# Attention chunks and a two-layer MLP on one core: v of the first batch loaded chunk by chunk, and the first loads and steps in another order

## The chip, the cores and the metric

The kernel runs on one core of one Trainium2 chip. The metric is device time in microseconds (us). A core has five engines that run side by side, each in the order of its own instructions: TensorE (PE: matrix products and transposes, written to PSUM banks), VectorE (DVE), ScalarE (ACT), GpSimd (POOL, here the issuer of nearly all loads) and SyncE (SP, here the issuer of stores and of DMA transposes). They meet through semaphores: an instruction that waits holds up all behind it on its engine. Loads and stores run on 16 DMA engines.

## The reference

```python
# q, k, v: 8 batches x 8 heads x 576 positions x 64, float32
q_c, k_c, v_c = (a.reshape(B, H, 9, 64, 64) for a in (q, k, v))    # chunks of 64 positions
scores = D ** -0.5 * np.matmul(q_c, k_c.transpose(0, 1, 2, 4, 3))
scores = scores - np.max(scores, axis=-1, keepdims=True)
attn = np.exp(scores)
attn = attn / (np.sum(attn, axis=-1, keepdims=True) + 1e-09)
out = np.matmul(attn, v_c)                                          # attention within a chunk only
x = out.transpose(0, 2, 1, 3).reshape(4608, 512)                    # tokens x (heads * 64)
h = x @ w_in                                                        # 512 x 2048
g = np.maximum(0.01 * h, h)
result = g @ w_out                                                  # 2048 x 512, float32
```

## The kernel before

**Attention units.** The 4608 tokens are cut into 36 units u of 128 tokens (two chunks, all 8 heads). A unit goes through stages, each a small function: `tq`/`tk` transpose q and k on PE, `q`/`k` (later `Q`) copy them from PSUM to SBUF, `s` computes the scores on PE, `m`/`b` take the row maximum and subtract it on DVE, `x` is the exponential on ACT, `z` the sum and its reciprocal, `n` the normalisation on DVE, `e`/`c` transpose the result on PE and copy it (u below 5) or `d` has it transposed by a DMA that SP issues (u of 5 and more), `v` multiplies with v on PE, and `a` copies the product to `xT` on ACT. From u=14 on q and k come as D loads and are transposed on DVE (`dq`, `dk`), and the exponential is fused with the subtraction (`nb`, `f`).

**MLP blocks.** The tokens are also cut into 22 blocks j: eight of 128 and fourteen of 256 tokens. The first layer `mm1(j, a)` (line 262) multiplies `w_inT` with `xT` into a PSUM bank `hT` (a pool of four banks), `act1` (stage G, line 277) puts the leaky ReLU into `gT`. The second layer is `mm2(j, ti, part)` (line 292, four matmuls of 512 columns) or, for blocks 8 to 20, seven half-size products `prod` with sums and differences of halves: `W` forms differences of `w_outT` (line 170) four times in all, `sum` those of `gT`, `comb` joins the products.

**Order.** Every engine's order is the order in which the Python code emits. Three texts and a list set it:

- `LOADS` is the order of the first loads, all issued by POOL on one queue: `gN` is q and k of unit N (lines 87), `vN` is v of batch N (two DMAs, line 109), `QN` a quarter of w_in (512 of its 2048 columns, two DMAs, line 116), `PN` a quarter of w_out (line 128). q and k of u=0 come on the queues of SP and ACT.
- `FRONT` is an order written out by hand for the first units and blocks. `iN` is filler: matmuls of `warm` with itself, N times 128 columns in pieces of up to 384. `yN`, `wN` zero parts of tiles, `I` copies the identity matrix. `Aj.a` is `mm1` of block j with w_in's quarter a, `Gj.a` its activation, `Bj.p` is `mm2` of block j with w_out's quarter p, `Oj` the copy and store of its result. A suffix such as `q1.0.1` names unit, half and engine (the last 1 is ACT).
- After `FRONT`, the remaining groups of matmuls (`chunks`) run one per step; ahead of each, all events due by that step are emitted, and all events up to the one that completes the tokens that the group needs. Event times follow from `T[u]`, the sum of `SPACE` up to u, and from distances: `O_P` (transposes ahead of scores), `O_Q` (DVE transposes ahead of scores), `O_X`, `O_N`, `O_Z` (exponential, normalisation behind scores), `O_U` (v behind scores for u below `U_V`) and `O_V` (from there on), `O_W` and `O_Y` (start and spacing of the four `W`), `O_E` and `O_L` (loads D3 and later), `O_D` (loads g9 to g13), `D_G` and its like for the MLP's own followers.
- v of batch b+2 is loaded into the tile of batch b right behind the last `v` that reads it (line 601's function calls `load_v`).

A load's place in `LOADS` is its place on POOL and on the queue. The tiles of v of the first batch, `VB[0]`, are read chunk by chunk: unit u reads chunks 2u and 2u+1, so u=0 reads 0 and 1, u=3 reads 6 and 7, and u=4 reads chunk 8 and the first chunk of batch 1.

Of the kernel before, what the change touches and what calls it, by code (L numbers as in the profile page):

```python
# [16 lines left out]
def kernel(  # L17
# [9 lines left out]
    nc = tc.nc  # L27

    B, H, S, D = q.shape
# [3 lines left out]
    CH = 64  # L33
# [25 lines left out]
    VB = [sbp.tile([128, H // 2, NCH, 128], FP16, name=f"VB{i}") for i in range(NVB)]  # L59
# [47 lines left out]
    def load_v(b):  # L107
        for m in range(2):
# [2 lines left out]
                in_=v[b, m * H // 2:(m + 1) * H // 2].rearrange("h (c j) d -> j (h c) d", j=CH),  # L111
            )

    def load_w_in(f0, f1):
        for m in range(2):
            nc.gpsimd.dma_start(
                out=w_inT[m * CH:(m + 1) * CH, :, f0:f1],
                in_=moe_w_in[m * d_model // 2:(m + 1) * d_model // 2, f0:f1].rearrange("(t d) f -> d t f", d=D),
            )

    def load_w_in_quarter(a):
        load_w_in(512 * a, 512 * a + 512)
# [11 lines left out]
    for eng, name, src in ((nc.sync, "q_f", q), (nc.scalar, "k_f", k)):  # L134
# [10 lines left out]
    qk[0] = tuple(first)  # L145

    LOADS = (
        "g2 g1 g3 v0 Q0 Q1 Q2 g4 Q3 g5 P1 P2 P0 P3 g6 v1 g7 g8 "
    )
    LOADERS = {"g": load_qk, "v": load_v, "Q": load_w_in_quarter, "P": load_w_out_quarter, "D": load_qk_batch}  # L150
    ident = sbp.tile([128, 128], FP16, name="ident")
    for n, what in enumerate(LOADS.split()):
        LOADERS[what[0]](int(what[1:]))
        if n == 0:
# [99 lines left out]
    def mm1(j, a, p):  # L254
        tb, c0 = part_of(j, p)
        r0 = (START[j] + c0) % RING
        nf = 512 // tb
        hT = psp.tile([128, nf, tb], FP32, name="hT", tag="mm", bufs=4)
        for i in range(nf):
            fc = nf * a + i  # L260
            for t in range(NT):
                nc.tensor.matmul(  # L262
                    out=hT[:, i, :],
                    lhsT=w_inT[:, t, fc * 128:(fc + 1) * 128],
                    rhs=xT[:, t, r0:r0 + tb],
                    start=(t == 0),
                    stop=(t == NT - 1),
                )
        HT[j, a, p] = hT
# [93 lines left out]
    def at(t, *what):  # L363
        now["order"] += 1
        events.append((t, now["order"], what))
        events.sort()
# [6 lines left out]
    def flush(*keys):  # L373

        for e in [e for e in events if e[2][0] in keys]:
            events.remove(e)
            issue(e)

    def later(n, *what):
        at(now["step"] + n, *what)  # L380

    def fill():
        kind, j, a, p = chunks.pop(0)
        if kind == "mm1":
            mm1(j, a, p)
            later(D_G, "G", j, a, p)
        elif kind == "sums":
            flush("G")
            for n, m in enumerate((1, 2, 3, 4)):
                later(n * D_S, "sum", j, m)  # L390
        elif kind == "prod":
# [5 lines left out]
            if p == BLOCKS[j] // 256 - 1:  # L397
                if a == 7:
                    later(D_K, "combX", j, 7)
                    later(D_K, "combZ", j, 5)  # L400
                elif a in (1, 6):
                    later(D_K, "combX", j, a)
                elif a == 4:
                    later(D_K, "combX", j, a)
                elif a == 2:
                    flush("combX")
                    later(D_C, "combW", j, a)
                elif a == 3:
                    later(D_C, "combZ", j, a)
        elif j == len(BLOCKS) - 1 and a == BLOCKS[j] // 128 - 1:  # L410
# [3 lines left out]
        else:  # L414
            flush("G")
            mm2(j, a, p)
            if parts[j, a] == NFC // 4:
                later(D_O, "O", j, a)

    D_G = 1.5  # L420
    D_S = 2.5
    D_K = 0.25
    D_C = 1.0
    D_O = 0

    QP: dict[int, bass.AP] = {}
    KP: dict[int, bass.AP] = {}
# [218 lines left out]
    def zero_act(i):  # L646
# [8 lines left out]
            )  # L655

    FRONT = (
        "i33 y4 y2 I y0 tq0 w3 q0.1.1 y1 tk0 k0 q0.0 i13 s0 m0 b0 tq1 q1.0.1 x0 tk1 q1.1 k1 i11 tq2 s1 z0 "
        "m1 b1 q2.0.1 tk2 q2.1.1 k2 x1 i5 tq3 n0 q3.0.1 i10 e0 c0.1 s2 tk3 z1 m2 v0 q3.1.1 a0 k3 n1 b2 "
        "i12 e1 c1 x2 i5 s3 v1 z2 a1 n2 m3 A0.0 G0.0 A1.0 e2 G1.0 A1.1 c2 v2 a2 b3 A0.1 A2.1 A1.2 x3 G1.1 "  # L660
        "z3 A2.0 G0.1 tq4 n3 G2.0 e3 tk4 c3 G2.1 A2.2 v3 G1.2 A0.2 A2.3 a3 G2.2 A1.3 q4.1 A3.3 G2.3 G0.2 "
        "A3.1 k4 G3.1 q4.0 G1.3 s4 G3.3 tk5 A3.2 y6 tq5 A3.0 m4 A0.3 G3.2 B1.2 G0.3 q5.0 b4 x4 B0.2 G3.0 "
        "B1.1 z4 B0.1 B1.0 B3.0 n4 k5.1 e4 B3.1 B1.3 B0.0 c4 B0.3 O1 q5.1.1 y5 O0 "
    )
    STAGES = {
        "tq": stage_tq, "tk": stage_tk, "q": stage_q, "k": stage_k, "s": stage_s, "m": stage_m, "b": stage_b,
# [25 lines left out]
            done.add((name, how[0]))  # L692
        STAGES[name](*how)

    SPACE = [4.5, 4.5, 5, 6.0, 6.0, 7, 4.5, 6, 6, 6, 7.5, 9.0, 8.5, 8.5, 9.5, 8.0, 7.5, 8.0, 7.0, 10.0, 7.0, 8.5, 7.5, 7.5, 8.5, 6.0, 8.0, 8.0, 9.0, 10.0, 9.0]
    O_P = 4.0
    O_Q = 6.5
    O_R = 1.0
    O_M = 0.5
    O_X = 3.0  # L700
    O_F = 3
    O_H = 0
    O_Z = 5.0
    O_N = 4.0
    O_U = 13.0
    O_V = 16.5
    U_V = 14
    O_L = -1.5
    O_W = 31
    O_Y = 2  # L710
    O_E = 2
    O_D = 4.0
    UY = 10
    T = {5: 0}
    for u in range(6, NU):
        T[u] = T[u - 1] + SPACE[u - 6]
    at(3, "v", 4)
    at(3, "a", 4)
    for u in range(5, NU):
        t = T[u]  # L720
        if u >= UD:
            at(t - O_Q, "dq", u, 0)
            at(t - O_Q + O_R, "dq", u, 1)
            at(t - O_Q + 2 * O_R, "dk", u)
        elif u > 5:
            for what in ("tq", "tk", "Q", "k"):
                at(t - O_P, what, u)
        at(t, "s", u)
        at(t + O_M, "m", u)
        if u < UX:  # L730
            at(t + O_M, "b", u)
            at(t + O_X, "x", u)
            n = t + O_N
        else:
            at(t + O_M, "nb", u)
            at(t + O_F, "f", u, 0, 4)
            at(t + O_F + O_H, "f", u, 4, 8)
            n = t + O_Z
        for what in ("z", "n", "d"):
            at(n, what, u)  # L740
        w = t + (O_U if u < U_V else O_V)
        at(w, "v", u)
        at(w, "a", u)
    for u in range(9, UD):
        at(T[u - 3] - O_D, "g", u)
    for b in range(3, B):
        at(T[9 * b // 2 - 5] - (O_E if b == 3 else O_L), "D", b)
    for n in range(4):
        at(O_W + n * O_Y, "W", n + 1)
    STAGES["Q"] = both  # L750
# [43 lines left out]
```

## Time and profile before

| what | us |
|---|---|
| median of 3 runs | 287.69 (287.58 to 287.98) |
| the profiled execution's own time | 287.43 |
| its span | 285.6 |
| PE busy | 275.5 (96%) |
| DVE busy | 198.3 (69%) |
| ACT busy | 197.3 (69%) |
| POOL busy | 115.2 (40%) |
| filler matmuls, 27 of 384 columns, 3 of 256, 2 of 128 | 8.4 |
| first-layer matmuls (line 262), 1408 | 142.9 |

The span is the time from the first to the last instruction of the profiled execution; its own time holds what lies around it as well. Busy time counts each engine's instructions; PE's includes the filler. A row of a timeline gives the start, the length, the engine, the line, the operation with the tiles it writes and reads, how many instructions are merged, and in brackets the idle time ahead with what ended it. Matmul lengths are modelled and overlap, so starts are the safer thing to count with.

### The profile page before, as it was taken

To read this page: it belongs to the slowest core of one execution; us is meant where nothing else is said; L and a number is where in the kernel's file an instruction comes from. 1 tells how busy PE (TensorE), PEld (TensorE's weight loads), DVE (VectorE), ACT (ScalarE), POOL (GpSimd) and SP (SyncE) were. 2 spreads that over 40 slices of the span, in tenths; PEclk is the share of its full clock that TensorE was granted. 3 is DMA by queue.
4 is the path that set the end of the run, shared out by engine and by line. 5 is a ranking of instruction groups with operands and counts; after the bars stand their busy time and mean duration, and the time that the engine had idled before them with its cause. 6 is when DMAs were issued, how large, how long until landed. Compare 5 with 4: busy or idle time off the path is not lost.

```text
span 285.6 us, 7842 instructions
## 1 busy us (share of the span) xinstructions
PE 275.5 (96%) x3140; PEld 233.8 (82%) x3140; DVE 198.3 (69%) x398; ACT 197.3 (69%) x634; POOL 115.2 (40%) x144
## 2 busy tenths in 40 slices
PE   8779999979999899999999999999999999999995
PEld 4569945777778799999999999999899999988874
DVE  5876245956699998787688886888787968442210
ACT  6856624646557697797788886878888888765431
POOL 8748625747899231963009830983000000000000
DMA  9999999999999939999919999999921212211012
GB/s 148 157 196 169 187 175 196 166 164 127 154 160 156 116 37 171 95 133 92 154 21 142 99 138 97 145 101 141 116 67 21 93 22 92 57 57 52 24 73 75
DMA packets 183332, 32.75 MB, mean 115 GB/s; under 512 B 174336, under 2 KB 178816, under 8 KB 183296
## 3 DMA queue, kind: packets, MB, share of 16 engines
q0 software_dynamic: 158880, 18.23, 121.4%
q1 hardware_dynamic: 23232, 13.70, 21.5%
q8 instruction: 24, 0.39, 0.5%
q10 hardware_dynamic: 1184, 0.33, 0.5%
q14 instruction: 12, 0.10, 0.1%
HBM read 36.96 MB, written 9.44 MB: 162 GB/s over the span
## 4 chain that ended last, share of the span: by engine, by line
PE 75%; DMA 12%; POOL 7%; DVE 4%; issue 1%; ACT 0%; DVEq 0%; ACTq 0%; POOLq 0%
PE hT L262 37%; PE prX L202 16%; PE prZ L202 8%; PE oP L292 5%; DMA q_d<-in_q_dram 5%; PE prW L202 4%; DMA w_inT<-in_moe_w_in_dram 3%; PE xp L601 2%; DMA et<-en 2%; DMA k_d<-in_k_dram 2%; PE Sp L507 2%; POOL k_d L100 2%; DVE TW L170 2%; POOL VB L109 2%; POOL k_in L87 1%; POOL q_in L87 1%
## 5 line engine op out<-in xcount | busy, mean ns | idle before, releaser
L262 PE MATMUL hT<-xT,w_inT 128*128 128x256 f16 (+1 forms) x1408 | 142.9, 253 | 2.0 <-DMA w_inT<-in_moe_w_in_dram 1.3
L262 PEld LDWEIGHTS <-w_inT 128*128 128x128 f16 x1408 | 115.0, 98 | 12.6 <-issue 2.4
L277 ACT ACTIVATE gT<-hT 128x512 f16<-128x512 f32 x144 | 84.4, 617 | 29.3 <-PE hT L262 28.6
L537 ACT ACTIVATE ex<-Sp,nb 128x64 f16<-128x64 f32 x176 | 52.5, 335 | 0.5 <-DVE nb L529 0.4
L100 POOL DMA_DIRECT2D q_d<-in_q_dram x40 | 32.4, 832 | 34.7 <-DVE QZ L489 29.2
L202 PEld LDWEIGHTS <-SG 128*128 128x128 f16 x416 | 40.4, 98 | 4.7
L537 ACT ACTIVATION_READ_ACCUMULATOR ex<-Sp,nb 128x1 f32 x176 | 40.3, 229 | 0.0
L516 DVE TENSOR_REDUCE mx<-Sp 128x8 f32<-128x512 f32 x36 | 24.7, 686 | 13.5 <-PE Sp L507 13.3
L100 POOL DMA_DIRECT2D k_d<-in_k_dram x40 | 32.4, 840 | 3.8 <-DMA q_d<-in_q_dram 3.5
L292 PE MATMUL oP<-w_outT,gT 128*128 128x512 f16 x144 | 33.5, 379 | 0.0
L615 ACT ACTIVATE xT<-xp 128x512 f16<-128x512 f32 x36 | 21.7, 602 | 16.9 <-PE xp L601 16.7
L202 PEld LDWEIGHTS <-gT 128*128 128x128 f16 x312 | 29.4, 98 | 3.2
L489 DVE STREAM_TRANSPOSE QZ<-q_d 64x512 f16<-64x512 f16 (+1 forms) x48 | 31.2, 656 | 0.4
L109 POOL DMA_DIRECT2D VB<-in_v_dram x16 | 18.5, 1168 | 29.6 <-PE xp L601 21.9
L227 DVE TENSOR_TENSOR osb<-prZ,keep 128x256 f32<-128x256 f32 x26 | 10.9, 418 | 25.7 <-ACT keep L218 14.8
L202 PE MATMUL prX<-TW,SG 128*128 128x256 f16 x208 | 27.0, 273 | 0.0
L568 DVE TENSOR_TENSOR en<-ex,zi 128x512 f16<-128x512 f16 x36 | 24.9, 691 | 1.2
L292 PEld LDWEIGHTS <-gT 128*128 128x128 f16 x144 | 13.3, 98 | 13.5
L218 ACT ACTIVATE keep<-prX 128x256 f32<-128x256 f32 x39 | 16.1, 412 | 8.3 <-PE prX L202 7.8
L561 DVE TENSOR_SCALAR ze<-z 128x8 f32<-128x8 f32 x36 | 8.8, 245 | 12.6 <-ACT ex L537 12.1
L183 DVE TENSOR_TENSOR SG<-gT 128x1024 f16<-128x1024 f16 x26 | 17.6, 675 | 0.0
L601 PEld LDWEIGHTS <-VB 128*128 128x128 f16 x288 | 13.0, 98 | 4.1 <-issue 2.3
(67 smaller groups left out, 312.1 us busy)
## 6 DMA issues: line engine op xcount, KB each, us to landing
out_dram<-osb SPq DMA_DIRECT2D x35, 256.0 KB, 3.1
VB<-in_v_dram POOLq DMA_DIRECT2D x16, 288.0 KB, 6.5
q_d<-in_q_dram POOLq DMA_DIRECT2D x40, 72.0 KB, 5.6
k_d<-in_k_dram POOLq DMA_DIRECT2D x40, 72.0 KB, 6.1
w_inT<-in_moe_w_in_dram POOLq DMA_DIRECT2D x8, 256.0 KB, 9.4
w_outT<-in_moe_w_out_dram POOLq DMA_DIRECT2D x4, 512.0 KB, 10.6
q_in<-in_q_dram POOLq DMA_DIRECT2D x11, 128.0 KB, 9.0
k_in<-in_k_dram POOLq DMA_DIRECT2D x11, 128.0 KB, 9.0
```

The costliest lines, as they stand in the source:

```text
L100: nc.gpsimd.dma_start(out=t[p0:p0 + 32, m, :, :, :].rearrange("p h b d -> p (h b) d"), in_=src[b, h0:h0 + 2, :, dh * 32:dh * 32 + 32].rear ...
L109: nc.gpsimd.dma_start(out=VB[b % NVB][m * CH:(m + 1) * CH, :, :, m * CH:(m + 1) * CH].rearrange("p h c d -> p (h c) d"), in_=v[b, m * H // ...
L202: nc.tensor.matmul(out=to[:, i, :], lhsT=left[:, f, i * 128:(i + 1) * 128], rhs=right[:, f, :], start=(j, where) not in opened, stop=(f == ...
L262: nc.tensor.matmul(out=hT[:, i, :], lhsT=w_inT[:, t, fc * 128:(fc + 1) * 128], rhs=xT[:, t, r0:r0 + tb], start=(t == 0), stop=(t == NT - 1),)
L277: nc.scalar.activation(out=gT[j][:, nf * a:nf * a + nf, c0:c0 + tb], in_=HT.pop((j, a, p)), func=AFT.Prelu, bias=0.0, scale=1.0, alpha=0.01,)
L292: nc.tensor.matmul(out=o, lhsT=gT[j][:, fc, ti * 128:(ti + 1) * 128], rhs=w_outT[:, fc, :], start=(n == 0 and fc == part * 4), stop=(n == ...
L489: nc.vector.transpose(out=qz[s * CH:(s + 1) * CH, :, e0:e0 + n, s, :], in_=qkd[b][0][s * CH:(s + 1) * CH, :, at:at + n * CH].rearrange("p ...
L516: nc.vector.tensor_reduce(out=MX[u], in_=SP[u], axis=AXL.X, op=ALU.max)
L537: nc.scalar.activation(out=E[u][:, i, :], in_=SP[u][:, i, :], func=AFT.Exp, bias=NB[u][:, i:i + 1], scale=SCL, accum_out=Z[u][:, i:i + 1],)
L568: nc.vector.tensor_tensor(out=E[u], in0=ex, in1=ZI.pop(u).unsqueeze(2).to_broadcast((128, 8, CH)), op=ALU.mult)
L601: nc.tensor.matmul(out=xp[:, t, e, :], lhsT=VB[b % NVB][:, t, c, :], rhs=et[:, t // 2, e, t % 2, :] if u < UD else et[:, t % 2, e, t // 2, :],
L615: nc.scalar.activation(out=xT[:, :, at:at + G], in_=xp, func=AFT.Copy, bias=0.0, scale=1.0)
```

## The change

One new loader takes a single chunk c of v of the first batch, two DMAs for it (one for each half of the heads). `LOADS` uses it nine times in place of `v0`, spread between the quarters of w_in, with chunk 8 behind v of batch 1; g3 stands behind the first quarter of w_in and three chunks, and the quarters of w_in and w_out come in another order. `FRONT` is written anew with the same stages: the number of filler units and their places differ (73 in place of 89), as does the order of zeroing, copies, first-layer and second-layer groups. Behind `FRONT`, `SPACE` and sixteen distances have other values. For u from 6 to 13, v comes 16.5 steps behind the scores in place of 13, since `U_V` is 6 in place of 14; for u=5 it is 12. The four `W` are due from step 14 on in place of 31, D3 at step 21 in place of 12.

```diff
+    def load_v_chunk(c):
+
+        for m in range(2):
+            nc.gpsimd.dma_start(
+                out=VB[0][m * CH:(m + 1) * CH, :, c, m * CH:(m + 1) * CH],
+                in_=v[0, m * H // 2:(m + 1) * H // 2, c * CH:(c + 1) * CH, :].rearrange("h j d -> j h d"),
+            )
+
     LOADS = (
-        "g2 g1 g3 v0 Q0 Q1 Q2 g4 Q3 g5 P1 P2 P0 P3 g6 v1 g7 g8 "
+        "g2 g1 c1 Q0 c2 c0 g3 Q2 c5 c3 Q1 c4 c7 Q3 g4 c6 g5 P3 P2 P1 P0 g6 v1 c8 g7 g8 "
     )
-    LOADERS = {"g": load_qk, "v": load_v, "Q": load_w_in_quarter, "P": load_w_out_quarter, "D": load_qk_batch}
+    LOADERS = {"g": load_qk, "v": load_v, "c": load_v_chunk, "Q": load_w_in_quarter, "P": load_w_out_quarter, "D": load_qk_batch}
-    D_G = 1.5
-    D_S = 2.5
-    D_K = 0.25
-    D_C = 1.0
-    D_O = 0
+    D_G = 1.25
+    D_S = 2.25
+    D_K = 0
+    D_C = 1.25
+    D_O = 0.75
     FRONT = (
-        "i33 y4 y2 I y0 tq0 w3 q0.1.1 y1 tk0 k0 q0.0 i13 s0 m0 b0 tq1 q1.0.1 x0 tk1 q1.1 k1 i11 tq2 s1 z0 "
-        "m1 b1 q2.0.1 tk2 q2.1.1 k2 x1 i5 tq3 n0 q3.0.1 i10 e0 c0.1 s2 tk3 z1 m2 v0 q3.1.1 a0 k3 n1 b2 "
-        "i12 e1 c1 x2 i5 s3 v1 z2 a1 n2 m3 A0.0 G0.0 A1.0 e2 G1.0 A1.1 c2 v2 a2 b3 A0.1 A2.1 A1.2 x3 G1.1 "
-        "z3 A2.0 G0.1 tq4 n3 G2.0 e3 tk4 c3 G2.1 A2.2 v3 G1.2 A0.2 A2.3 a3 G2.2 A1.3 q4.1 A3.3 G2.3 G0.2 "
-        "A3.1 k4 G3.1 q4.0 G1.3 s4 G3.3 tk5 A3.2 y6 tq5 A3.0 m4 A0.3 G3.2 B1.2 G0.3 q5.0 b4 x4 B0.2 G3.0 "
-        "B1.1 z4 B0.1 B1.0 B3.0 n4 k5.1 e4 B3.1 B1.3 B0.0 c4 B0.3 O1 q5.1.1 y5 O0 "
+        "y0 y4 i46 I tq0 w3 tk0 q0.1.1 y1 y2 k0 q0.0 s0 m0 tq1 q1.0.1 tk1 k1 b0 x0 q1.1 tq2 z0 s1 q2.1.1 m1 "
+        "b1 q2.0.1 i3 tk2 k2 x1 tq3 i7 i13 n0 q3.0.1 e0 tk3 s2 i2 c0.1 z1 m2 k3 v0 b2 q3.1.1 i2 n1 s3 a0 x2 "
+        "m3 e1 c1 z2 v1 a1 n2 A0.0 b3 A1.0 e2 G1.0 A1.2 x3 c2 v2 G0.0 A1.1 A0.1 z3 n3 a2 A2.1 G1.2 e3 G0.1 "
+        "c3 A2.0 G1.1 tk4 v3 A2.2 k4 A0.2 tq4 G2.0 a3 A3.3 A2.3 q4.1 A3.0 A1.3 G2.1 A3.1 G0.2 G2.2 q4.0 s4 "
+        "A0.3 G3.3 G2.3 m4 G1.3 b4 G3.1 A3.2 B1.3 B1.2 B1.1 y6 G0.3 x4 tq5 B3.1 G3.0 B0.3 B1.0 B0.2 z4 y5 n4 "
+        "tk5 e4 q5.1.1 O1 G3.2 B3.0 k5.1 B0.0 q5.0 B0.1 c4 O0 "
     )
-    SPACE = [4.5, 4.5, 5, 6.0, 6.0, 7, 4.5, 6, 6, 6, 7.5, 9.0, 8.5, 8.5, 9.5, 8.0, 7.5, 8.0, 7.0, 10.0, 7.0, 8.5, 7.5, 7.5, 8.5, 6.0, 8.0, 8.0, 9.0, 10.0, 9.0]
-    O_P = 4.0
-    O_Q = 6.5
-    O_R = 1.0
-    O_M = 0.5
-    O_X = 3.0
+    SPACE = [4.5, 5.5, 5, 5.5, 6.0, 5.0, 4.5, 5, 5.5, 7.5, 8.5, 8.5, 6.0, 10.5, 10.5, 8.0, 7.0, 8.0, 7.5, 9.5, 7.0, 8.5, 8.0, 6.0, 7.5, 6.5, 10.0, 8.0, 6.0, 9.0, 11.5]
+    O_P = 3.5
+    O_Q = 6.0
+    O_R = 1.25
+    O_M = 0
+    O_X = 1.0
-    O_Z = 5.0
-    O_N = 4.0
-    O_U = 13.0
+    O_Z = 6.0
+    O_N = 3.0
+    O_U = 12.0
     O_V = 16.5
-    U_V = 14
-    O_L = -1.5
-    O_W = 31
-    O_Y = 2
-    O_E = 2
-    O_D = 4.0
+    U_V = 6
+    O_L = -5.0
+    O_W = 14
+    O_Y = 3.5
+    O_E = -6
+    O_D = 5.5
```

## The prediction

> **What bounds the kernel now.** I read the page first: TensorE (PE) is busy 96% of a span of 285.6 us, at a granted clock of 1.00. Then I read PE's own timeline for the places where it is not fed, because a PE-bound kernel can only change there or in its amount of work. The page:
>
> ```profile
> span 285.6 us, 7842 instructions
> PE 275.5 (96%) x3140; PEld 233.8 (82%) x3140; DVE 198.3 (69%) x398; ACT 197.3 (69%) x634; POOL 115.2 (40%) x144
> ...
> DMA packets 183332, 32.75 MB, mean 115 GB/s; under 512 B 174336, under 2 KB 178816, under 8 KB 183296
> ```
>
> PE's timeline, front (start us, us, what; the bracket is idle time and who ended it):
>
> ```profile
> 16.58 0.39 PE L601 MATMUL xp<-et,VB 128*128 128x64 f16 x8
> 18.23 1.95 PE L262 MATMUL hT<-xT,w_inT 128*128 128x128 f16 x32 [1.25 <-DMA w_inT<-in_moe_w_in_dram]
> ...
> 25.09 0.39 PE L441 MATMUL qp<-ident,q_in 128*128 128x128 f16 x4
> ...
> 26.65 0.40 PE L601 MATMUL xp<-et,VB 128*128 128x64 f16 x8
> ```
>
> The first matmul of the first layer (call its start A0) is at 18.23 us; before it PE runs transposes, scores and filler matmuls on `warm`. From there it is fed almost without a gap. The exceptions:
>
> ```profile
> 54.60 2.75 PE L292 MATMUL oP<-w_outT,gT 128*128 128x512 f16 x12
> 58.78 0.39 PE L601 MATMUL xp<-et,VB 128*128 128x64 f16 x8 [1.43 <-DMA et<-en]
> ```
> ```profile
> 87.33 3.92 PE L262 MATMUL hT<-xT,w_inT 128*128 128x256 f16 x32
> ...
> 93.07 0.40 PE L601 MATMUL xp<-et,VB 128*128 128x64 f16 x8
> 94.15 1.03 PE L262 MATMUL hT<-xT,w_inT 128*128 128x256 f16 x8 [0.69 <-ACT xT L615]
> ...
> 97.00 1.04 PE L202 MATMUL prW<-w_outT,gT 128*128 128x256 f16 x8
> 98.11 0.41 PE L601 MATMUL xp<-et,VB 128*128 128x64 f16 x8
> ```
>
> The reader can size each gap from starts: twelve 512-column matmuls start every 216 ns, so those of 54.60 are through at 57.19 and the next starts at 58.78: 1.59 lost. Thirty-two 256-column ones at 109 ns from 87.33 would be through at 90.83, the next starts at 91.09: 0.27. 93.07 to 94.15 holds eight at 29 ns: 0.85. 97.00 to 98.11: 0.24. Together 2.95 us, and no other gap over 0.15 us until the end. So the time is A0, plus a fixed amount of PE work, plus such gaps, plus the tail after the last matmul.
>
> Last, POOL's timeline, which issues all loads of the front in order on one queue:
>
> ```profile
> 5.94 2.33 POOL L109 DMA_DIRECT2D VB<-in_v_dram  x2
> 8.21 3.75 POOL L116 DMA_DIRECT2D w_inT<-in_moe_w_in_dram  x6
> 12.30 0.69 POOL L87 DMA_DIRECT2D q_in<-in_q_dram  x1 [0.34 <-DMA VB<-in_v_dram]
> 14.75 0.68 POOL L87 DMA_DIRECT2D q_in<-in_q_dram  x1 [1.75 <-DMA VB<-in_v_dram]
> ...
> 20.54 0.61 POOL L116 DMA_DIRECT2D w_inT<-in_moe_w_in_dram  x1 [0.62 <-DMA w_inT<-in_moe_w_in_dram]
> ```
> ```profile
> DMA to landing us min/median/max: 7.0/7.0/7.0
> ```
>
> POOL idles here for the landing of an earlier load: its ninth load in flight waits for the first of the eight before. The last row is the transfer issued at 20.54 (second half of the last quarter of w_in): it lands at 27.52. By their landings the loads finish in the order of issue: g1 at 8.51, g3 at 10.09, v0 at 12.02 and 14.47, then w_in halves about 1.3 us apart. The queue is full from about 4 us on.
>
> **The change part by part.** The profiled execution took 287.43 us, 1.83 us more than its span and 0.26 below the median of 287.69. I change the span and add the difference to 287.69. The amount of PE work from A0 on is unchanged: the same products, transposes and scores, in another order.
>
> *1. Filler matmuls.* 89 units of 128 columns become 73, all before A0. The first block grows from 33 to 46. In the trace 384 columns take 320 ns until 4.5 us and 163 ns later, so the five extra ones end at about 5.5 us instead of 4.87; the scores of u=0 follow 0.65 later. Nothing is charged for this if the loads come later still, which is part 2.
>
> *2. Order of the first loads.* The new order is g2 g1 c1 Q0 c2 c0 g3 Q2 c5 c3 Q1 c4 c7 Q3 g4 c6 g5, where c is one chunk (two DMAs) of v of the first batch. A chunk's transfer: v0's halves took 1.93 and 2.45 us by landings, so a ninth of both is 0.49 us. Its issue is not shown: 0.61 us a DMA as for w_inT (L116, also 256 rows each) is the nearest row, against 1.17 for half of v0. Sixteen chunk DMAs before or at c6 make 9.8 us of POOL time, where v0 took 2.3. The 7.5 us more fall on 6.9 us that POOL idles between 12 and 25 us (the brackets above and those between them): they just about fit, and c6 is issued near 24 us, three before it lands.
>
> Two landings matter. First g3: behind g1 (8.51) now come c1 0.49, Q0 2.55, c2 and c0 0.98, and its own first half 0.78, so about 13.3 us in place of 9.29. PE's order puts tq3 ahead of the transpose e0 and the scores of u=2. Hence: tq3 at 13.3, then 20 filler units (1.1) and e0 to 14.9, tk3 0.4, scores of u=2 at 15.5, maximum and subtraction on DVE 0.44+1.4, scores of u=3 at 17.35, e1 0.6 later behind n1, c1 behind m3 at 18.85, v1, and A0 at about 19.15. The 1.25 us that PE waited for w_in at 18.23 is gone, since Q0 lands near 12, and yet A0 is 0.9 later.
>
> Second c6, which v3 (the u=3 product with v) needs. Ahead of and with c6, the queue carries exactly what before carried up to the landing at 27.52, less c8: 27.0 us. From A0 to v3 PE has seven groups of 16 matmuls at 56 ns (6.25) and four small groups (0.9): 7.2 us. So v3 is ready at 26.35 but starts at 27.15, as if A0 had been 19.95. Against 18.23 that is +1.7 us for everything behind. This is the term that I take. Its low end is +0.9 (c6 not late, only g3). Its high end comes from the chunk's price: if a chunk DMA takes 0.61 in the queue rather than 0.24, sixteen add up to 5.9, of which the two to four us of w_in ahead in the queue hide most; I keep +3.5. I stay by 0.24 because a chunk has the same 256-byte rows as v0.
>
> The w_out quarters come behind g5 as before, less c8: first about 31.3, last 40.0 us. Their first users stand at 35.9 and 40.4 with the shift, so they add nothing; with c6 two us later they move along.
>
> *3. The wait at 57 us.* It is v5 waiting for the DMA transpose of u=5, issued at 50.78 and landed at 58.74. That issue was late because the exponential x5 stood behind v4 and its copy on ACT:
>
> ```profile
> 48.42 0.69 DVE L559 TENSOR_REDUCE z<-ex 128x8 f32<-128x512 f16 x1 [2.23 <-ACT ex L550]
> ...
> 50.00 0.69 DVE L568 TENSOR_TENSOR en<-ex,zi 128x512 f16<-128x512 f16 x1
> ```
>
> Now x5 stands at step 1, ahead of v4 (step 3), so the sum can follow the copies that end at 46.19 instead of 48.42: 2.2 us earlier, while v5 itself is 0.9 earlier (step 12, not 13). Of 1.59 about 0.3 stays: -1.3, bounds -1.6 and 0.
>
> *4. Weight differences (W, four of 1.2 us on DVE)* move from steps 31 to 37 to steps 14 to 25, from the stretch where DVE is busy 96% (80 to 100 us) to one at 60 to 73%. The gaps of 0.27 and 0.24 follow late DVE work there and should go: -0.5, bounds -0.5 and 0. The 0.85 at 93.07 stays: v11 still stands directly ahead of the first matmul that reads its columns, and copy and wait take 1.08 from v to that matmul.
>
> *5. Lag of v, loads D3, the distances.* For u from 6 to 13, v comes 16.5 steps after the scores, not 13: transposes get 11 to 14 us in place of 8 to 9.5. In exchange v6 stands one group (1.1 us) ahead of its reader, just the 1.08 needed, and v9 1.55. Later the distance from scores to v is at least 13.8 us; the trace needs 5.7 to 7.4 to the transpose's issue and 2.4 to 6.4 to land. D3's 16 DMAs go behind g12 and g13 on POOL, whose buffers wait for tq8 (step 12), so they start near 61 us, not 53; at some 0.95 each they land by 82, and their reader is due near 87. v3's batch load and D4 behind them lose nothing, as D4 is first read near 113. I add +0.1 for all this, bounds 0 and +0.8.
>
> Sum: +1.7 -1.3 -0.5 +0.1 = 0.0: 287.7 us. A measurement of this kernel can tell about 0.2% (0.57 us) from no change.
>
> The Trainium skill (DMA: Bandwidth & Descriptors, "Anatomy of one DMA") gives each DMA from POOL a fixed cost of about 2 us beside its bytes. By that rule the chunks would be the worst of the change: eight in flight would give an estimated 0.25 us a DMA, hardly above my 0.24; alone, not overlapped, sixteen would add an estimated 32 us. The landings 0.8 us apart (g2 to g3) say that the cost overlaps, so the rule moves neither sum nor chance.
>
> **Rivals.**
>
> *Faster: the loads do not hold PE.* If c6 and g3 land about 2 us earlier than I count, for instance because much of the lag between a load's share of the queue and its landing (27.52) belongs to w_in's large rows, then A0 is set by Q0 no more: tq3 could go at 12.0 after the copies of u=2, A0 at 17.9, no wait at v3. Front -0.3, total -2.0: 285.7. Against it: bytes ahead of c6 are those of before. For it: the second half of Q0 landed 2.3 us after the first and the next one 0.9 after that, so a landing is not the load's own share alone.
>
> *Slower: POOL becomes the bound of the front.* With at most eight loads in flight, six or eight of them small, the queue runs dry between quarters of w_in, c6 lands at 28.5 to 29.5 and v3 waits 2 us and more: front +3.5, total +1.8: 289.5. It decides from c6 at 27.6 on (net +0.6). For it: 7.5 us of new issue time against 6.9 of idle time. Against: a third of these issues lies under quarters that take 2.6 us each.
>
> *No gain at 57 us.* The transpose lands late anyway, since v5 is 0.9 earlier too: +1.3, 289.0.
>
> **How the numbers follow.** Even trade: 0.38, 287.7, own range 286.9 to 288.5. Loads not binding: 0.30, 285.7. POOL-bound or no gain at 57: 0.32, 289.0 to 289.5. Of the even trade a fifth lies below 287.1 and a fifth above 288.3. Faster 0.38, within 0.2% 0.23, slower 0.39. The range runs from 285.4 to 289.6.
>
> **What would show it.** A0 near 19.2 with PE's wait on `w_inT` gone; PE waiting on q_in of u=3 near 12 to 13 and on VB near 26.5; no `et` wait over 0.5 near 58; TW at 60 to 75 us; 0.85 still lost ahead of the first matmul of block 9. The prediction is wrong if `xp` never waits for VB, if POOL shows no idle time from 5 to 25 us, or if gaps appear behind 100 us.

## The result, and the profile after

The changed kernel takes 291.5 us (290.38 to 292.17, four runs) against 287.84 for the kernel before: ratio 1.0114, interval 1.0068 to 1.0160. It is slower by 1.1%, and outside the range forecast (285.4 to 289.6). The profiled execution took 291.74 us with a span of 289.7, against 287.43 and 285.6.

The page of the changed kernel, first rows of its parts 1 and 2:

```profile
span 289.7 us, 7857 instructions
...
PEclk9656999999999999999999999999999999999999
...
DMA packets 183588, 32.75 MB, mean 113 GB/s; under 512 B 174592, under 2 KB 179072, under 8 KB 183552
```

The row `PEclk` is the one that matters: TensorE's granted clock, in tenths, in 40 slices of 7.24 us. From the second to the fourth slice it is well below 9. The trace of before has no record of a clock change at all, and its filler matmuls start at the full rate from 4.5 us on; the prediction never asks what keeps the clock there.

PE's timeline up to 34 us (start, length, line, operation, count, and in brackets the idle time ahead and who ended it):

```profile
8.32 0.41 PE L515 MATMUL Sp<-KT,QZ 128*128 128x64 f16 x8 [0.96 <-DVE QZ L476]
...
10.99 0.64 PE L454 MATMUL qp<-ident,q_in 64*64 64x64 f16 x16 [1.65 <-DVE QZ L476]
...
14.19 0.64 PE L454 MATMUL qp<-ident,q_in 64*64 64x64 f16 x16 [1.13 <-DMA q_in<-in_q_dram]
14.76 2.32 PE L631 MATMUL idle<-warm 128*128 128x384 f16 x8
...
20.21 0.59 PE L515 MATMUL Sp<-KT,QZ 128*128 128x64 f16 x8 [0.75 <-DVE sh L528]
...
21.91 0.59 PE L609 MATMUL xp<-et,VB 128*128 128x64 f16 x8 [0.58 <-DMA VB<-in_v_dram]
22.30 3.60 PE L270 MATMUL hT<-xT,w_inT 128*128 128x128 f16 x32
...
31.43 0.39 PE L449 MATMUL kp<-ident,k_in 128*128 128x128 f16 x4
31.65 0.40 PE L609 MATMUL xp<-et,VB 128*128 128x64 f16 x8
```

A0, the first matmul of the first layer, is at 22.30 us (18.23 before, 19.15 forecast). tq3 waits for q of u=3 at 14.19, as forecast in kind. Two more waits of PE stand ahead of it, 0.96 at 8.32 and 1.65 at 10.99, for copies (`QZ`) on DVE. Before, filler stood in those places, `i13` and `i11` (rows of the kernel before):

```profile
5.95 0.87 PE L623 MATMUL idle<-warm 128*128 128x384 f16 x5
6.80 0.40 PE L507 MATMUL Sp<-KT,QZ 128*128 128x64 f16 x8
...
8.92 0.77 PE L623 MATMUL idle<-warm 128*128 128x384 f16 x4
9.79 0.44 PE L446 MATMUL qp<-ident,q_in 64*64 64x64 f16 x16
```

The 20 filler units at 14.76 take until 16.86, where the prediction had 1.1 us, and 32 first-layer matmuls at 22.30 take 3.40 us to the next start, where 32 of them otherwise take 1.8. The bracket at 21.91 names VB, but the last chunk that this product reads had landed by 19.58; what it waited for is the copy of `et` that DVE ended at 21.85. v3 at 31.65 has no bracket: it comes right behind tk4.

The same, by windows of 3.41 us (columns: window, its length, PE busy and instructions, granted clock, DMA share, GB/s):

```profile
core 0: us, PE busy (x), PEclk, DMA share, GB/s
3.02:6.43 3.41, 3.41 (x14) 1.00 1.65 209
6.43:9.84 3.41, 1.96 (x48) 1.00 1.33 123
9.84:13.25 3.41, 2.06 (x41) 0.50 1.67 172
13.25:16.66 3.41, 2.47 (x23) 0.50 1.11 145
16.66:20.08 3.42, 2.80 (x40) 0.50 1.38 151
20.08:23.49 3.41, 2.70 (x32) 0.50 1.36 146
23.49:26.90 3.41, 3.41 (x35) 0.50 1.39 165
```

The records of the clock begin at 6.42 us, so the first row's 1.00 has none behind it; its filler matmuls of 384 columns start every 0.32 us, which is half rate (0.163 at full). From 9.84 to 26.90 us, five such windows, the clock is 0.50 by the records. This begins behind the window in which PE was busy for 1.96 us of 3.41.

The loads, in POOL's timeline:

```profile
7.03 2.53 POOL L117 DMA_DIRECT2D VB<-in_v_dram  x4
...
11.48 0.63 POOL L124 DMA_DIRECT2D w_inT<-in_moe_w_in_dram  x1 [0.56 <-DMA w_inT<-in_moe_w_in_dram]
12.73 0.61 POOL L124 DMA_DIRECT2D w_inT<-in_moe_w_in_dram  x1 [0.62 <-DMA w_inT<-in_moe_w_in_dram]
...
17.53 0.61 POOL L117 DMA_DIRECT2D VB<-in_v_dram  x1 [0.51 <-DMA w_inT<-in_moe_w_in_dram]
18.96 1.83 POOL L117 DMA_DIRECT2D VB<-in_v_dram  x3 [0.82 <-DMA w_inT<-in_moe_w_in_dram]
...
25.16 1.28 POOL L117 DMA_DIRECT2D VB<-in_v_dram  x2
```
```profile
DMA to landing us min/median/max: 4.3/4.3/4.3
```

A chunk DMA keeps POOL for 0.60 us from one start to the next, and four of them take 2.53. The second quarter of w_in is issued at 11.48, where the first's first half has just landed (11.20): the eight loads ahead of it were both halves of that quarter, four chunk DMAs and q and k of u=3. What was in flight by then was small: q and k of u=3 have landed by 14.82, and the first half of the next quarter lands at 17.24, 2.4 us behind them, where a half in a full queue takes 1.3. The first halves of the next two quarters, each behind four chunk DMAs, land 2.0 and 1.8 us behind the load ahead of them. The last row is the transfer issued at 25.16, first half of c6: 4.3 us to landing, 29.42; its second half lands at 29.64 (27.0 forecast).

Further back, the places that lost time before (rows of PE):

```profile
62.21 0.39 PE L449 MATMUL kp<-ident,k_in 128*128 128x128 f16 x4
62.44 0.40 PE L609 MATMUL xp<-et,VB 128*128 128x64 f16 x8
...
97.50 0.40 PE L609 MATMUL xp<-et,VB 128*128 128x64 f16 x8
98.84 1.03 PE L270 MATMUL hT<-xT,w_inT 128*128 128x256 f16 x8 [0.95 <-ACT xT L623]
```

v5 at 62.44 stands directly behind its neighbour: its transpose landed 1.53 us earlier. The gaps of 1.59, 0.27 and 0.24 are gone; the one ahead of block 9 is there, 1.11 by starts (0.85 before). No gap follows.

So the spans add up like this. A0 is 4.07 later. From A0 to v3 it takes 9.35 us, where the same work at full clock is 7.15 by the prediction's count: 2.2 more. The gaps give back 1.59 + 0.27 + 0.24 - 0.26 = 1.84. Together +4.4; the spans differ by 4.1, and 0.3 is spread over small steps.

### The profile page after: what moved, and what is told of

Same layout as the page of the kernel before. It is cut to its first block, busy times and chain, and to the rows that moved or that the text cites. A ratio compares the mean times of both kernels' runs of the same rounds, so it can differ in the third digit from the quotient of the medians.

```text
span 289.7 us, 7857 instructions
## 1 busy us (share of the span) xinstructions
PE 279.4 (96%) x3135; PEld 238.2 (82%) x3135; DVE 198.8 (69%) x398; ACT 196.9 (68%) x634; POOL 123.7 (43%) x160
## 3 DMA queue, kind: packets, MB, share of 16 engines
q0 software_dynamic: 159136, 18.23, 116.7%
## 4 chain that ended last, share of the span: by engine, by line
PE 88%; DMA 5%; POOL 2%; DVE 2%; ACT 1%; issue 1%; DVEq 0%; ACTq 0%; POOLq 0%
PE hT L270 42%; PE prX L210 16%; PE oP L300 11%; PE prZ L210 8%; DMA w_inT<-in_moe_w_in_dram 4%; PE prW L210 4%; PE xp L609 3%; PE Sp L515 2%; PE oP L326 1%; ACT gT L285 1%; DMA VB<-in_v_dram 1%; PE qp L449 1%; PE kp L449 1%; POOL VB L117 1%; POOL k_in L87 0%
## 5 line engine op out<-in xcount | busy, mean ns | idle before, releaser
L270 PE MATMUL hT<-xT,w_inT 128*128 128x256 f16 (+1 forms) x1408 | 145.8, 256 | 0.9 <-ACT xT L623 0.9
L270 PEld LDWEIGHTS <-w_inT 128*128 128x128 f16 x1408 | 117.5, 99 | 11.6 <-issue 1.0
L109 POOL DMA_DIRECT2D VB<-in_v_dram x14 | 16.1, 1162 | 29.9 <-PE xp L609 17.0
L235 DVE TENSOR_TENSOR osb<-prZ,keep 128x256 f32<-128x256 f32 x26 | 10.9, 420 | 25.3 <-ACT keep L226 15.0
L515 PE MATMUL Sp<-KT,QZ 128*128 128x64 f16 x288 | 14.9, 197 | 1.7 <-DVE QZ L476 1.0
```

The costliest lines, as they stand in the source:

```text
L270: nc.tensor.matmul(out=hT[:, i, :], lhsT=w_inT[:, t, fc * 128:(fc + 1) * 128], rhs=xT[:, t, r0:r0 + tb], start=(t == 0), stop=(t == NT - 1),)
L515: nc.tensor.matmul(out=Sp[:, i, :], lhsT=qz[:, 2 * m + g, e, :, :], rhs=kt[:, 2 * m + g, e, :], start=True, stop=True)
```

## The experiments

Two theories stood at first. *Clock*: the filler that went (ahead of s0, tq2 and tq3) had kept the granted clock up, and its absence costs the time. *Loads*: the new order, with v in chunks, brings g3, w_in and c6 too late. Each ratio below is against runs of the kernel before on the same chip, with its 95% interval.

**e1_filler: the three removed pieces of filler put back into the changed kernel.**

```diff
-... k0 q0.0 s0 m0 ... q1.1 tq2 z0 ... k2 x1 tq3 i7 i13 ...
+... k0 q0.0 i13 s0 m0 ... q1.1 i11 tq2 z0 ... k2 x1 i10 tq3 i7 i13 ...
```

> The changed kernel with filler added where its PE waited: 13 units ahead of the scores of u=0, 11 ahead of tq2, 10 ahead of tq3; nothing else. Theory 'clock' (the waits let PE's granted clock fall to 0.5 from 9.8 to 26.9 us, and that is all of the loss): clock 1.00, A0 from 22.3 to about 19, time 287 to 288. Theory 'loads' (the new order of loads holds PE whatever its clock): clock 1.00 and A0 near 19.5, but v3 waits for chunk 6 until about 29.7 us, where the changed kernel started it at 31.65, so only about 1.9 us come back: 289.6. Rival 'distances' (the loss lies behind the front): 291.5, no change.

Measured: 291.85 us, ratio 1.0150 (1.0109 to 1.0190). PE of this run:

```profile
15.62 0.63 PE L454 MATMUL qp<-ident,q_in 64*64 64x64 f16 x16 [3.71 <-DMA q_in<-in_q_dram]
```

The filler held the clock at 1.00 to 14.52 us instead of 9.84, and then PE waited 3.71 us for q of u=3, a window with only 0.80 us of PE work went by, and the clock was 0.50 up to 28.18. The execution shown was an unlucky one: q landed at 15.58, where the same loads gave 14.14 in the changed kernel's trace, and it took 293.16 us at a mean clock of 0.976, the other three 291.63 to 292.01 at 0.988 to 0.994. Those three lost less to the clock than the changed kernel (0.971 to 0.982) and were no faster. Filler without the loads is worth nothing here: what is not lost at half clock is lost in waits for loads.

**e2_less_filler: the kernel before, without `i13` ahead of s0 and `i11` ahead of tq2.**

```diff
-... q0.0 i13 s0 m0 ... k1 i11 tq2 s1 ...
+... q0.0 s0 m0 ... k1 tq2 s1 ...
```

> The kernel before without two of its fillers, the 13 units ahead of the scores of u=0 and the 11 ahead of tq2; all else as before. Theory 'clock': PE's granted clock falls to 0.5 for some stretch of the front, mean 0.97 to 0.99, time 289 to 292. Theory 'loads' or 'distances': the fillers lie in waits, so 287.8, within 0.3, clock 1.00.

Measured: 288.9 us, ratio 1.0062 (1.0032 to 1.0092). The windows of this run:

```profile
4.80:8.21 3.41, 2.08 (x33) 1.00 1.73 165
8.21:11.62 3.41, 2.46 (x68) 0.50 2.20 150
11.62:15.03 3.41, 3.41 (x44) 0.50 1.59 165
```

Less filler alone takes the clock down, in a kernel whose loads are untouched: the mean clock was 0.981 to 0.994 in all ten executions, and 0.999 or more in 13 of the 15 of the kernel before. The time is just under the 289 to 292 expected. A0 moved by only 0.25 us (18.48), since the load of w_in sets it there; 1.0 us more went into the wait for the transpose of u=5, 2.58 by starts, ending at 60.42 (1.59 before).

**e3_loads: the kernel before with the new `LOADS` alone.**

```diff
-        "g2 g1 g3 v0 Q0 Q1 Q2 g4 Q3 g5 P1 P2 P0 P3 g6 v1 g7 g8 "
+        "g2 g1 c1 Q0 c2 c0 g3 Q2 c5 c3 Q1 c4 c7 Q3 g4 c6 g5 P3 P2 P1 P0 g6 v1 c8 g7 g8 "
```

> The kernel before with the new order of first loads alone (chunks of v, g3 behind Q0): the hand-written order, filler and distances are those of before. Theory 'loads': tq3 waits for g3 until about 14.2 us, not 11.8, A0 near 20, v3 waits for chunk 6 until about 29.7 where it started at 26.65: 290 to 291. Theory 'clock' alone: the fillers are all there, 287.8 within 0.5, unless the wait for g3 itself lets the clock fall, which the granted clock would show below 1.00.

Measured: 295.07 us, ratio 1.0244 (1.0201 to 1.0288). The waits that show it:

```profile
14.43 0.64 PE L454 MATMUL qp<-ident,q_in 64*64 64x64 f16 x16 [2.67 <-DMA q_in<-in_q_dram]
...
28.90 0.39 PE L449 MATMUL qp<-ident,q_in 128*128 128x128 f16 x4 [1.08 <-DMA q_in<-in_q_dram]
...
43.18 5.08 PE L300 MATMUL oP<-w_outT,gT 128*128 128x512 f16 x15 [2.29 <-DMA w_outT<-in_moe_w_out_dram]
```

tq3 waits 2.67 for g3 and A0 is at 20.58; tq4 waits for g4. The time is above the 290 to 291 expected. A part of that is the wait that ends at 43.18, which is a mismatch, and not the changed kernel's: the old order asks for quarters of w_out in the order 2, 0, 1, the new loads bring 3, 2, 1, 0.

**e4_dist: the kernel before with the new `SPACE` and distances alone.** The old `LOADS` and `FRONT` stay; `SPACE`, all fourteen values that change below `FRONT` and the five `D_` values are in (nineteen in all, where the text on the change says sixteen).

> The kernel before with the new spaces and distances alone: loads and hand-written order are those of before. By the trace of the changed kernel the gaps of 1.59, 0.27 and 0.24 us are gone and the one ahead of block 9 is about 1.1 in place of 0.85: 286.0, with 285.7 to 286.6. Rival 'distances cost': 288.5 and more. Theories 'clock' and 'loads' have no say here, as A0 should stay at 18.2.

Measured: 285.3 us, ratio 0.9907 (0.9872 to 0.9942), clock 0.999. With e10_dist_v11, below, this is the fastest of all, and it beats both kernels. PE:

```profile
56.86 0.39 PE L441 MATMUL kp<-ident,k_in 128*128 128x128 f16 x4
57.08 0.40 PE L601 MATMUL xp<-et,VB 128*128 128x64 f16 x8
...
92.14 0.40 PE L601 MATMUL xp<-et,VB 128*128 128x64 f16 x8
93.43 1.03 PE L262 MATMUL hT<-xT,w_inT 128*128 128x256 f16 x8 [0.89 <-ACT xT L615]
```

v5 no longer waits, and the 0.27 and 0.24 are gone; the wait ahead of block 9 stays. Parts 3 to 5 of the prediction are seen here by themselves: they gain 2.1 us by the medians and 2.7 by the ratio (interval 1.7 to 3.7), where 1.7 was forecast. In this execution A0 was at 17.73, 0.50 earlier than in the trace of before, with the front unchanged, so a part of the difference may be the landing of loads. By the ratios (1.0114 and 0.9907) the loads and the front together cost 2.1%, about 6 us.

**e5_whole_v: the changed kernel with v whole again.**

```diff
-        "g2 g1 c1 Q0 c2 c0 g3 Q2 c5 c3 Q1 c4 c7 Q3 g4 c6 g5 P3 P2 P1 P0 g6 v1 c8 g7 g8 "
+        "g2 g1 g3 v0 Q0 Q2 Q1 Q3 g4 g5 P3 P2 P1 P0 g6 v1 g7 g8 "
```

> The changed kernel with v of the first batch loaded whole again and g3 ahead of it: g2 g1 g3 v0 Q0 Q2 Q1 Q3 g4 g5, then the w_out quarters in the changed order; hand-written order and distances stay as changed. Theory 'loads' (chunks and the late g3 are the loss, through PE's waits, the clock and chunk 6): g3 lands near 10.1, A0 near 18.3 to 19.3 (some cold clock stays, since the fillers are thin), v3 about 7.2 us later at 25.5 to 27.5 where the changed kernel has 31.65: 286 to 288. Rival 'hand-written order' (the thin filler and the order themselves cost): 290 and more.

Measured: 288.89 us, ratio 0.9993 (0.9961 to 1.0026). A0 is at 20.36, v3 at 29.59. Against 1.0114 with chunks, loading v whole (with g3 ahead of it, as before) is worth 1.2%; the spans of the two profiled executions differ by 2.0 us. The clock still falls, from 11.05 to 24.71. Q3 stays ahead of g4, as in the changed kernel and unlike before; e12_whole_v_g4 turns that round.

**e6_g3_early: the changed kernel with g3 ahead of c1; e7_g3_filler: that, with `i13` and `i11` put back.**

```diff
-        "g2 g1 c1 Q0 c2 c0 g3 Q2 ...
+        "g2 g1 g3 c1 Q0 c2 c0 Q2 ...
```

> The changed kernel with one load moved: g3 stands behind g1, ahead of chunk 1 and Q0; the chunks stay. Theory 'g3' (the wait of tq3 for g3 is what stops PE and halves its clock): A0 from 22.3 to 18.5 to 20, clock 0.98 to 1.00. Then either chunk 6, landing at 29.6 as in the changed kernel, holds v3 (from 31.65 to 29.8: 289.5), or, if it does not, 287.5. Rival 'filler' (the clock falls before tq3 because of thin filler): clock stays near 0.975, 291 to 292.

> As the one with g3 early, and 13 units of filler ahead of the scores of u=0 and 11 ahead of tq2, as the kernel before has. Theory 'clock and chunk 6': clock 1.00, A0 18 to 18.5, and PE then waits at v3 for chunk 6 (29.6): 289.4, hardly less than without the filler. Theory 'clock alone': 286.5 to 287, the full gain of the distances.

Measured: 291.22 us, 1.0094 (1.0053 to 1.0135), A0 21.32, v3 29.91; and 290.7 us, 1.0082 (1.0044 to 1.0120), A0 19.93, v3 30.40. Neither can be told from the changed kernel (1.0068 to 1.0160). In e6_g3_early tq3 no longer waits (it starts at 13.55), and the clock falls all the same, from 10.67 to 17.50 and again from 20.91 to 24.32: here it is the waits that lost their filler, and not the wait for g3, that take it down. Set beside e5_whole_v, which has g3 in the same place, it also shows what the chunks cost by themselves: 1.0094 against 0.9993, 1.0%. In e7_g3_filler the clock holds to 17.70 and is 0.50 to 24.53. A0 is 2.4 us earlier than in the changed kernel, and little of it arrives:

```profile
17.94 0.37 PE L609 MATMUL xp<-et,VB 128*128 128x64 f16 x4 [0.60 <-DMA VB<-in_v_dram]
...
19.75 0.37 PE L609 MATMUL xp<-et,VB 128*128 128x64 f16 x4 [1.44 <-DMA VB<-in_v_dram]
...
29.92 0.38 PE L449 MATMUL kp<-ident,k_in 128*128 128x128 f16 x4 [0.70 <-DMA k_in<-in_k_dram]
```

The second half of v1 waits 1.44 us for chunk 3, which landed at 19.62. (The bracket of 0.60 names VB too, but chunk 2 had landed by 14.34; what ends it is the copy of `et`, as in the changed kernel.) tk4 waits for g4, which the chunks hold up, v3 comes just behind c6 (landed at 30.27), and the second layer waits for w_out at 40 and 43 us. With g3 early and the filler back, loads behind or among the chunks are the next wait at each place.

**e8_chunks_in_place: the kernel before with v0 as nine chunks in its old place.** This measures a chunk's price.

```diff
-        "g2 g1 g3 v0 Q0 Q1 ...
+        "g2 g1 g3 c0 c1 c2 c3 c4 c5 c6 c7 c8 Q0 Q1 ...
```

> The kernel before with v0 replaced by its nine chunks in the same place (c0 to c8 between g3 and Q0); nothing else. The price of eighteen small loads for two. If a chunk costs its 0.24 us in the queue: Q0 lands at 18.1 as before, 287.8 within 0.3. If POOL's 0.6 us an issue is the price: eighteen take 10.8 us, the last is issued near 17, Q0 lands near 21 to 22, A0 three us late, PE waits without filler and its clock falls too: 291 to 293.

Measured: 295.95 us, ratio 1.0225 (1.0152 to 1.0298). POOL, and PE behind it:

```profile
5.94 11.08 POOL L117 DMA_DIRECT2D VB<-in_v_dram  x18
16.85 3.84 POOL L124 DMA_DIRECT2D w_inT<-in_moe_w_in_dram  x6
```
```profile
22.99 3.57 PE L270 MATMUL hT<-xT,w_inT 128*128 128x128 f16 x32 [5.96 <-DMA w_inT<-in_moe_w_in_dram]
```

Eighteen DMAs keep POOL for 10.9 us, where the two of v0 took 2.3. The first five, still behind other loads, land 0.2 us apart, and the other thirteen 0.6 us apart in the mean, at the pace of issue. Q0 is issued at 16.85 and lands at 21.55 and 22.85 (15.8 and 18.1 before), and PE waits 5.96 us. The price is POOL's, as the second case expected, and the time is above its 291 to 293. In the changed kernel, where chunks queue behind quarters of w_in, they land 0.16 to 0.28 us apart. So the same load costs about 0.22 us where something large covers its issue, and 0.60 where nothing does.

**e9_whole_v_filler: e5_whole_v with `i13` and `i11` put back. e10_dist_v11 and e11_front_v11: e4_dist and e9_whole_v_filler with v of u=11 four steps earlier.**

```diff
-        w = t + (O_U if u < U_V else O_V)
+        w = t + (O_U if u < U_V else O_V) - (4 if u == 11 else 0)
```

> As the one with v loaded whole in the changed kernel, and 13 units of filler ahead of the scores of u=0 and 11 ahead of tq2, nothing else. Theory 'clock' (what is left of the loss there, some 2.5 us against the kernel before with the new distances, is PE at a clock of 0.5 from 11.0 to 24.7 us because the front's waits lost their filler): clock 0.995 to 1.00, A0 from 20.4 to 18.0 to 18.5, time 2 to 3 us under the same kernel without the filler, at 0.990 to 0.994 of the kernel before. Rival 'order' (the hand-written order itself is slower): clock 1.00 and yet 0.998 to 1.00 of before.

> The kernel before with the new spaces and distances, and v of u=11 four steps earlier, so that it no longer stands directly ahead of the first matmul of block 9. If the 1.05 us lost there is PE waiting for the copy to xT: gone, 0.987 to 0.989 of the kernel before, about 1 us under the one with the distances alone. If the transpose of u=11 lands too late for it: the wait moves to v11 and at most 0.3 us is won.

> As the changed kernel with v whole and the filler, and v of u=11 four steps earlier. About 1 us under the one without that step, and level with the kernel before with the new distances and the same step, within 0.5 us, if neither hand-written order is the better one.

Measured: 288.2 us, 0.9990 (0.9961 to 1.0018); 285.61 us, 0.9896 (0.9865 to 0.9928); 288.34 us, 0.9989 (0.9962 to 1.0016). In e9_whole_v_filler A0 is at 18.29 and the clock is down only from 18.05 to 21.46, but tk4 waits 1.37 at 28.26 for g4, behind Q3; so the 2 us won at A0 shrink to nothing measurable against e5_whole_v, which is where rival 'order' had put it. The step of v11 is a miss twice: the wait ahead of block 9 only moves to other places (0.83 by starts, up to 91.03, in e10_dist_v11; 1.00, up to 93.38, in e11_front_v11).

**e12_whole_v_g4: e5_whole_v with g4 ahead of Q3 again. e13_all_filled: that, with filler in every wait of the front.** These two ran on one chip and differ in filler alone.

```diff
+        "g2 g1 g3 v0 Q0 Q2 Q1 g4 Q3 g5 P3 P2 P1 P0 g6 v1 g7 g8 "
-... q0.0 s0 ... q1.1 tq2 ... x1 tq3 i7 i13 ... q3.1.1 i2 n1 s3 ... z2 v1 ...
+... q0.0 i13 s0 ... q1.1 i11 tq2 ... x1 i10 tq3 i7 i13 ... q3.1.1 i17 n1 s3 ... z2 i10 v1 ...
```

> As the changed kernel with v whole, but g4 ahead of the last quarter of w_in, as in the kernel before; no filler added. It is the base for the next one. Theory 'clock': PE at 0.5 for ten us and more of the front, mean clock 0.976 to 0.988, A0 near 20.4, 0.998 to 1.000 of the kernel before.

> The same with filler in each wait that PE's timeline showed: 13 units ahead of the scores of u=0, 11 ahead of tq2, 10 ahead of tq3, 15 more ahead of the scores of u=3, 10 ahead of v1. The work, the loads and the order are those of the kernel beside it. Theory 'clock': clock 0.998 to 1.00, A0 18.0 to 18.7, 2 us and more under the kernel beside it, 0.989 to 0.993 of the kernel before. Rival 'order': clock 1.00, and yet within 0.5 us of the kernel beside it, since its waits only moved into filler.

Measured: 289.2 us, 1.0034 (1.0006 to 1.0061), and 287.63 us, 0.9990 (0.9961 to 1.0019). The `PEclk` rows of the two pages, in this order:

```profile
PEclk9757999999999999999999999999999999999999
```
```profile
PEclk9999999999999999999999999999999999999999
```

With 59 more units of filler, which do no work, the kernel is 1.6 us faster: A0 at 18.57 for 20.11, v3 at 27.00 for 29.33. The mean clock is 0.999 or 1.00 in eleven of twelve executions, and 0.976 to 0.988 in all twelve without this filler. That is the clock's price here, less than the 2 us and more expected. Not all of the 2.33 us won at v3 arrives, because PE now meets loads:

```profile
22.99 2.84 PE L270 MATMUL hT<-xT,w_inT 128*128 128x128 f16 x48 [1.11 <-DMA w_inT<-in_moe_w_in_dram]
...
38.42 1.02 PE L300 MATMUL oP<-w_outT,gT 128*128 128x512 f16 x4 [0.80 <-DMA w_outT<-in_moe_w_out_dram]
```

The first is A1.1, whose quarter Q1 landed at 22.85 behind Q2; the second is w_out's P1. What is left between this kernel and e4_dist is 1.7 us of span: A0 0.84 later (18.57 for 17.73), and by starts 0.86 more in waits for w_in and w_out (2.24 for 1.38). That comes from the two traces; no run takes the waits away.

The kernel before shows something of the clock's price with nothing edited. Of its 91 executions beside these runs, the mean clock was below 0.998 in 24, and in the mean these took 0.8 to 1.9 us longer than the others on the same chip. Loads that happen to land late could cause both, so this is no price by itself; it does say that the filler of before keeps the clock up in most executions, not in all.

**What the runs come to**, step by step from before to the changed kernel: the distances alone -0.9% (e4_dist); the new front on top, with v whole, +0.9% (e5_whole_v), or +1.3% with g4 in its place (e12_whole_v_g4), of which filler wins back 0.4 (e13_all_filled); the chunks, with g3 behind three of them, +1.2%, to 1.0114. The steps come from different chips, and each ratio's interval is 0.3 to 0.5% either way. So the clock is the smaller part of the front's cost where it could be measured alone, and 0.8% is left with the clock at 1.00 (e13_all_filled against e4_dist); that this is the order in which the front asks for loads is read from traces, not tried alone.

## Why the prediction was wrong

*Part 1, filler: wrong, a term put at nothing.* "Nothing is charged for this if the loads come later still" costs the filler by its own length. What it also did was hold the clock (e2_less_filler, e13_all_filled). In the changed kernel there are 16 units fewer, and 13 more of the rest stand in the first block, where they fill none of the later waits: PE stood idle 0.96 and 1.65 us ahead of tq3, and then came half clock to 26.90. Of A0's 3.15 us over the forecast, 0.89 is tq3 (14.19 for 13.3) and 2.26 the stretch from tq3 to A0 (8.11 us for 5.85), of which the filler block is 1.0. The 2.2 us from A0 to v3 are the clock's too. The prediction took the clock of before, a state that the filler helped to keep, for a constant. In this one trace most of the miss is thus time at half clock, but the runs do not make it the larger term: filler put back wins nothing while loads hold PE (e1_filler, e9_whole_v_filler) and 1.6 us at most (e13_all_filled), and v loaded whole wins 1.2%, 3.5 us.

The first block of filler was mis-timed too. It was to end at about 5.5 us, at full rate from 4.5 on as in the trace of before; it ran at half rate throughout and ended at 6.2, since the clock rose only at 6.42. With the same first block, e5_whole_v and e12_whole_v_g4 had it at 4.23 and 3.96, so the moment differs from one execution to the next.

*Part 2, order of loads: right in kind, the time of the quarters mis-sized.* g3 was late and tq3 waited, as written. "I stay by 0.24 because a chunk has the same 256-byte rows as v0" held: the sixteen chunk DMAs up to c6 took 3.5 us of landings, where eight ninths of v0 is 3.9. What failed is the step behind it, that the queue "carries exactly what before carried" and so takes the same time. The four quarters of w_in took 14.2 us of landings for 10.9 before, because, by POOL's rows, they were issued behind the chunks and behind landings, and c6 came at 29.64 for 27.0. For g3 the same error could have been read from the trace of before: the sum had 2.55 for Q0, which took 3.62 there (14.47 to 18.09) and 3.84 here. The rival "POOL becomes the bound of the front" had this (c6 28.5 to 29.5, 289.5 in total). It was nearest among the rivals, though not for its own reason at v3: PE reached v3 later than c6 did. The price of POOL shows in e8_chunks_in_place and in e7_g3_filler. The range ended at 289.6 because its upper end priced late loads alone; no term of the sum had the clock.

*A0 and v3.* Wait on `w_inT` gone: right. A0 near 19.2: wrong by 3.1. `xp` waiting for VB near 26.5: wrong, since PE was too late to wait; by the prediction's own criterion ("wrong if `xp` never waits for VB") this step fell.

*Part 3, wait at 57 us: right.* All 1.59 went, -1.3 forecast. The rival "no gain at 57 us" fell.

*Part 4, weight differences: right.* 0.27 and 0.24 went; 0.85 stayed, as 1.11.

*Part 5, lag of v: right.* +0.1 forecast, no gap behind 100 us; the four `W` run from 65 to 78 us, as forecast (60 to 75) but for the last. e4_dist measures parts 3 to 5 together: 0.9907, about 2.1 to 2.7 us against the forecast sum of 1.7. The rival "the loads do not hold PE" fell with part 2.

## What to carry to other kernels

A filler matmul is costed by the clock it holds, not by its length, and it wins nothing where a load ends the wait anyway: where a change moves waits of PE, count PE's busy time in each 3.4 us window ahead and behind, and ask of each window that is less than two thirds full what the same matmuls cost at half clock. Splitting a load that is not too large pays only if the issuer has time: price each small DMA at the issue's duration (0.60 us here) unless a longer transfer certainly covers it, and ask what the large load behind it loses by being issued later. And when one edit bundles several, run the parts: here one part gains 0.9% and the others lose 2%.

## What the runs showed of the hardware

In these traces the granted clock has two values, 1.00 and 0.50, and changes only at the ends of windows of 3.41 us, whose phase differs from run to run (the first rise was at 3.96 to 7.28 us). I counted PE's busy time in each window of the fronts of all runs with such records. The clock fell behind 14 windows, with 0.00 to 2.08 us busy (1.96 in the changed kernel, 0.80 in e1_filler, 1.95 in e12_whole_v_g4); it held behind all with more than 2.10 and, up to 50 us, behind four of 1.92 to 2.10. Later it also held behind windows as thin as 1.79 (e3_loads, from 64.0 us) and 2.02 (e2_less_filler, from 56.0). Once it had fallen to 0.50, it rose behind windows busy for 2.97 us or more, most of them full, and not behind those of 1.74 to 3.06, four of which stand in the table of the changed kernel. So every fall stands behind a window that is at least 39% idle, and every rise behind one that is nearly full, and a front at the edge loses many windows for one that is thin. Busy times are modelled, and the ranges overlap: some windows as idle cost nothing. What else in a window counts, and whether all kinds of matmul count alike, is open.

The Trainium skill (TensorE: Matmul & The Clock Gate, "Part 1: The HAM clock gate") has the half rate as the default and a free-running activity window of 3413 ns that sets it; the 0.50 and the 3.41 us agree. The same page ("HAM oscillation — how this bites in real kernels") gives as a rule that PE must have no idle gap over about 3.4 us. Here the measurement decides otherwise: the gaps of the changed kernel around its fall at 9.84 us were 0.96 and 1.65 us.

For small loads, the Trainium skill (DMA: Bandwidth & Descriptors, "Anatomy of one DMA") puts a fixed 2 us on each DMA from POOL. In e8_chunks_in_place the last thirteen of eighteen small ones land 0.6 us apart in the mean, so that cost overlaps, and what does not is POOL's time to issue.
